# Block-sparse attention in the last batch of an attention-then-gMLP kernel, with key blocks and value rows gathered by register addresses

## The chip, the cores and the metric

The kernel runs on one core of one Trainium2 chip. The metric is device time in microseconds (us) of one execution, as the median of the runs shown. "Span" is the time from the first to the last instruction in one profiled execution. The engines go by the profile's names: PE (TensorE; PEld are its weight loads), DVE (VectorE), ACT (ScalarE), POOL (GpSimd), SP (SyncE, which here only issues DMAs).

## What is computed

Attention of 4 batches with 8 heads each (768 positions, 64 values a head) under a mask made of blocks of 32 positions, and behind it a gMLP block whose spatial product mixes all 768 positions of a batch. There are 24 query blocks and 24 key blocks:

```python
B, H, S, D = q.shape                       # 4, 8, 768, 64
mask = np.abs(blk_i - blk_j) <= 1
mask = mask | (blk_i == 0) | (blk_j == 0) | (blk_i == n_blocks - 1) | (blk_j == n_blocks - 1)
for qb in range(n_blocks):
    for kb in sampled_blocks[qb]:          # 3 drawn block numbers for each query block
        mask[qb * block:(qb + 1) * block, kb * block:(kb + 1) * block] = True
scores = np.where(mask, scale * np.matmul(q, k.transpose(0, 1, 3, 2)), -1e9)
attn = softmax(scores)                     # exp, divided by its sum
x = np.matmul(attn, v)                     # heads side by side: 4 x 768 x 512
h = np.maximum(x @ w_in, 0.0)              # d_ff = 1024
u, v = h[..., :512], h[..., 512:]
v_n = (v - mean(v)) / np.sqrt(var(v) + 1e-06)
v_s = np.einsum('ts,bsd->btd', w_spatial, v_n) + b_spatial[None, :, None]
out = (u * v_s) @ w_out
```

An inner query block may look at its own block and its two neighbours, at the first and the last key block, and at three drawn blocks: 8 of the 24, fewer where some coincide. The first and the last query block look at all 24. The drawn numbers are an input, so they are known only on the chip.

## The kernel before

**Staging.** Heads are worked in pairs: pair p is batch p // 4, heads 2(p % 4) and the next, so batch b has pairs 4b to 4b + 3. `load` (line 106) brings k, q and v of a pair from memory on SP's queue as [128, 2, 384] fp32; `cast` (118) turns them to bf16 on POOL, v into `vv`; `tr_dma` (372) transposes the pair's k and q with one DMA transpose on SP; `split` (376) copies one head from there into `kq[head]` on DVE. `kq` (line 83) holds 8 heads of keys and queries, 64 rows of values and under them rows that carry the mask: a product of keys and queries adds the penalty of a forbidden block by itself, so all 24 key blocks are computed for each query block.

**Slots.** An order written out by hand runs over slots s (loop at line 846). Batch 0 takes slots 0 to 35 in another form. From slot 36 (`S0`) on, each slot does one `qk_full` (422): for one head and one chunk of 128 keys, two products into PSUM (512 and 256 queries, line 428) and one exp on ACT over 128 x 768 (431) into the tile `a_all`. Seven slots later (`LAG`) `av_full` (471) multiplies: six products of 65 columns (values and a column of ones) for one chunk of 128 queries (line 476). A pair takes 12 slots, `slot_of(p) = 36 + 12 (p - 4)`; so the last batch, pairs 12 to 15, has slots 132 to 179. After six chunks `normalize` (438) divides on DVE; `xtr_dma` (507) transposes the pair's result by DMA on SP, after which the gMLP can read it.

**gMLP.** The gMLP of batch b (class `Moe`, 571) is a list of 108 steps, each one product of 512 columns or two of 256: 48 for `in_steps`, 36 for the spatial product, 24 for the last one. `deal` and `run_queue` spread it over 48 slots. Batch 2's list starts at slot 144, inside the last batch's attention; batch 3's runs alone at the end (line 867). In `v_product` DVE computes mean and variance, POOL the reciprocal root (`std`, `rstd`, lines 598 and 600), and DVE scales `vn` with it; the spatial product reads `vn`. `o_product` (669) issues the output DMA on SP (682).

**Order.** `when(slot, ...)` puts work into a slot (lines 808 to 837). Each engine's queue is in program order; a wait holds all that stands behind it on that engine. SP carries all loads, DMA transposes and outputs. A DMA waits until the one eight places before it, which uses the same semaphore, has landed.

Of the kernel before, what the change touches and what calls it, by code (L numbers as in the profile page):

```python
# [26 lines left out]
def kernel(  # L27
# [16 lines left out]
    nc = tc.nc  # L44
# [27 lines left out]
    psum = ctx.enter_context(tc.tile_pool(name="psum", bufs=1, space=bass.MemoryType.PSUM))  # L72
    ctx.enter_context(tc.manual_schedule())
# [8 lines left out]

    kq = const.tile([128, H, 2 * S], BF16, name="kq")
    NVV = 6
    vv = [const.tile([128, 2, NCH, VA], BF16, name=f"vv{s}") for s in range(NVV)]
# [20 lines left out]
    def load(p, nm, hs=BOTH, cs=ALLC, eng=nc.sync):  # L106
        if (nm, p) not in st:
            st[nm, p] = work.tile([128, 2, S // 2], FP32, tag="st_" + nm, bufs=4 if nm == "q" else 3, name="st_" + nm)
        eng.dma_start(out=st[nm, p][:, hs, cs.start * D:cs.stop * D],
                      in_=dram(SRC[nm], p, hs, cs))  # L110
# [7 lines left out]
    def cast(p, nm, eng, hs=BOTH, cs=ALLC):  # L118
        if nm == "v":
            dst = vv[p % NVV][:, hs, cs, 0:D]  # L120
        else:
            if p not in nat:
                nat[p] = work.tile([128, 2 * NCH, 2, D], BF16, tag="nat", bufs=4, name="nat")
            c0 = 0 if nm == "k" else NCH
            dst = nat[p][:, c0 + cs.start:c0 + cs.stop].rearrange("p c h d -> p h c d")[:, hs]
        src = st[nm, p].rearrange("p h (c d) -> p h c d", d=D)[:, hs, cs]
        if p == 0 and nm != "v":
            dst = nat0_view()[:, hs, (c0 + cs.start) * D:(c0 + cs.stop) * D]
            if cs is not C45:
                dst = dst[:, 0].rearrange("p (i t d) -> p t i d", t=2, d=D)  # L130
                src = src[:, 0].rearrange("p (t i) d -> p t i d", t=2)
            else:
                dst = dst.rearrange("p h (c d) -> p h c d", d=D)
        if eng is nc.scalar:
            nc.scalar.activation(out=dst, in_=src, func=AF.Copy)
        else:
            eng.tensor_copy(out=dst, in_=src)  # L137
# [13 lines left out]
    hot = const.tile([128, NCH, 128], BF16)  # L151
    lim = const.tile([128, NCH, 128], BF16)
# [65 lines left out]

    def w_load(key, src):
        wst[key] = work.tile([128, DM], FP32, tag="osb", bufs=6, name="w_f")  # L220
        nc.sync.dma_start(out=wst[key], in_=src)
# [160 lines left out]


# [3 lines left out]
    def qk_unit(u, e):  # L387
        if e == 0:
            a_ref[u] = work.tile([128, NCH * S], BF16, tag="a_all", bufs=3,
                                 name="a_all")[:, 0:2 * NCH * TW]  # L390
# [31 lines left out]
    def qk_full(j, ci):  # L422
        if ci == 0:
            a_ref["h", j] = work.tile([128, NCH * S], BF16, tag="a_all", bufs=3,
                                      name="a_all").rearrange("p (c n) -> p c n", c=NCH)
        ps = psum.tile([128, 1024], FP32, tag="sc", bufs=2)
        for n0, n1 in ((0, 512), (512, S)):
            nc.tensor.matmul(out=ps[:, n0:n1],  # L428
                             lhsT=kq[:, j % H, ci * 128:(ci + 1) * 128],
                             rhs=kq[:, j % H, S + n0:S + n1], start=True, stop=True)  # L430
        nc.scalar.activation(out=a_ref["h", j][:, ci, :], in_=ps[:, 0:S], func=AF.Exp, scale=0.125)  # L431
# [80 lines left out]

    ws = {}

    def ws_load(i):
        ws["f", i] = work.tile([128, S], FP32, tag="ws_f", bufs=6, name="ws_f")
        nc.sync.dma_start(out=ws["f", i],
                          in_=moe_w_spatial.rearrange("(p c) s -> c p s", c=NCH)[i])

    def b_load():  # L520
        ws["b_nat"] = work.tile([128, S], FP32, tag="ws_f", bufs=6, name="b_nat")
        nc.sync.dma_start(out=ws["b_nat"], in_=moe_b_spatial.partition_broadcast(128))
# [5 lines left out]
    def ws_cast(i):  # L528
        if i % 2 == 0:
            ws["b", i // 2] = work.tile([128, 2, NCH, 128], BF16, tag="ws_b", bufs=2, name="ws_b")  # L530
# [40 lines left out]
    class Moe:  # L571
# [97 lines left out]
        def o_product(self, tcc, n):  # L669
# [4 lines left out]
            for i in range(parts):  # L674
                cs = slice(i * w, (i + 1) * w)

                def done(ps, i=i, cs=cs):
                    if i == 0:
                        osb["t"] = work.tile([128, DM], FP32, tag="osb", bufs=6, name="osb")
# [105 lines left out]
    def last_x():  # L785
# [13 lines left out]
        xt = xt_tile(NP - 1)  # L799
        for cs in (slice(0, TW), slice(TW, S)):  # L800
            dve_copy(xt[:, cs], ps[:, cs])
# [9 lines left out]
    for p in range(NG, NP):  # L811
        g = slot_of(p)
        when({4: 14, 5: 20, 6: 28, 11: g - 29, 15: g - 29}.get(p, g - 36), c(load, p, "k"), c(load, p, "q"), c(load, p, "v"))
        when({4: 17, 5: 23, 6: 37, 11: g - 22, 15: g - 22}.get(p, g - 24),
             *[c(cast, p, nm, PL, cs=cs) for nm in "kqv" for cs in (((C01, C23, C45) if p > 5 else (ALLC,)))])
        when({4: 21, 5: 27, 11: g - 18, 15: g - 18, 10: g - 17, 14: g - 17}.get(p, g - 19), c(tr_dma, p))
# [5 lines left out]
        if p == NP - 1:  # L822
            when(g + 20, last_x)
        elif p % NG == NG - 1:
# [13 lines left out]

    LAG = 7
    av_at = {}  # L840
# [5 lines left out]
    for s in range(NS + LAG + 2):  # L846
        if s < S0:
            qk_unit(*divmod(s, 3))
        elif s < NS:
# [7 lines left out]
        if 0 <= s - LAG - S0 and s - LAG < NS:  # L857
# [40 lines left out]
```

## Time and profile before

| what | value |
|---|---|
| runs (us) | 210.04, 210.03, 210.24; median 210.04 |
| span of the profiled execution | 208.3 us, granted clock 1.000 |
| the execution's own time | not on the page; 210.04 - 208.3 = 1.7 us is taken as what lies around the span |
| busy share of the span | PE 97%, PEld 66%, DVE 70%, ACT 81%, POOL 43% |
| DMA | 53053 packets, 39.48 MB, mean 190 GB/s |

A busy PE means that some matmul is under way; matmuls are pipelined, so the time that one costs is read from start to start. In a group's row "busy" is the union of its instructions, "mean ns" the length of one. Rows with "SPq" are instructions of SP's own sequencer: their length is the time for which the queue is held. A row of one line's instructions gives min/median/max in ns and the first and last start in us.

### The profile page before, as it was taken

The numbers are of one execution on the slowest core, as the hardware profiler recorded it, in microseconds if no ns is written. First come the engines' busy times: TensorE is split into PE (matmuls) and PEld (weight loads), VectorE is DVE, ScalarE is ACT, GpSimd is POOL, SyncE is SP. The second block draws the span as 40 slices with busy tenths as digits, with TensorE's granted clock in tenths as the row PEclk, the third lists the DMA queues.
The fourth block names the chain that finished last, engine by engine and source line by source line (L and its number), as shares of the span: only waits on it lengthen the run. The fifth ranks groups of instructions, "written<-read, shape, count | busy, mean of one in ns | idle before, by whom it ended". The sixth has DMA issues, their size and how long they took to land.

```text
span 208.3 us, 5489 instructions
## 1 busy us (share of the span) xinstructions
PE 201.0 (97%) x2203; PEld 138.0 (66%) x2225; DVE 146.8 (70%) x315; ACT 168.4 (81%) x222; POOL 89.4 (43%) x186
## 2 busy tenths in 40 slices
PE   6899999999999999999999999999999999999993
PEld 6599888777766776667556676667665567445551
DVE  6888776989876766575975585456875666576871
ACT  6899999999999999989899878889899884266021
POOL 6888989767927964006757600006210000013000
PEclk9999999999999999999999999999999999999999
DMA  5999899999999999499987920499402010610016
GB/s 143 338 362 357 275 383 270 206 247 389 253 253 308 259 300 208 139 199 386 292 176 206 139 41 0 164 189 335 75 0 41 0 37 4 250 57 0 0 70 232
DMA packets 53053, 39.48 MB, mean 190 GB/s; under 512 B 33956, under 2 KB 47652, under 8 KB 53028
## 3 DMA queue, kind: packets, MB, share of 16 engines
q1 hardware_dynamic: 52596, 38.74, 70.0%
q10 hardware_dynamic: 432, 0.39, 0.6%
q8 instruction: 17, 0.28, 0.5%
q14 instruction: 8, 0.07, 0.1%
HBM read 24.77 MB, written 6.29 MB: 149 GB/s over the span
## 4 chain that ended last, share of the span: by engine, by line
PE 87%; DVE 4%; ACT 4%; DMA 2%; issue 1%; POOL 0%; ACTq 0%
PE ps L428 21%; PE ps_moe L630 17%; PE ps_moe L561 13%; PE ps_av L476 12%; PE ps L415 7%; PE ps_av L458 4%; PE ps_t L561 4%; PE ps_t L630 4%; PE ps_sc L630 2%; ACT a_all L420 2%; DVE stats L594 2%; DVE vn L185 2%; DMA st_q<-in_q_dram 2%; PE ps_sc L561 1%; PE ps L263 1%
## 5 line engine op out<-in xcount | busy, mean ns | idle before, releaser
L431 ACT ACTIVATE a_all<-ps 128x768 bf16<-128x768 f32 x144 | 113.4, 812 | 13.8 <-PE ps L428 6.2
L428 PE MATMUL ps<-kq 128*128 128x512 bf16 (+1 forms) x288 | 70.3, 326 | 0.3
L476 PEld LDWEIGHTS <-a_all 128*128 128x128 bf16 x864 | 46.6, 98 | 19.0
L476 PE MATMUL ps_av<-vv,a_all 128*128 128x65 bf16 x864 | 51.1, 194 | 0.1
L428 PEld LDWEIGHTS <-kq 128*128 128x128 bf16 x288 | 27.9, 97 | 23.6
L137 POOL CAST nat<-st_k 128x256 bf16<-128x256 f32 (+3 forms) x37 | 17.7, 509 | 38.7 <-DMA st_k<-in_k_dram 38.7
L420 ACT ACTIVATE a_all<-ps 128x1024 bf16<-128x1024 f32 x35 | 33.5, 1027 | 0.3
L630 PE MATMUL ps_moe<-w_spt,vn 128*128 128x512 bf16 (+1 forms) x144 | 33.1, 325 | 0.0
L598 POOL TENSOR_SCALAR std<-mv 128x3 f32<-128x3 f32 (+1 forms) x9 | 3.4, 376 | 48.7 <-DVE mv L595 48.5
L661 DVE TENSOR_TENSOR sb<-ps_moe,b_row 128x512 f32<-128x512 f32 x18 | 12.4, 690 | 14.5 <-PE ps_moe L630 14.2
L630 PE MATMUL ps_moe<-xt,w_in_t 128*128 128x256 bf16 (+1 forms) x108 | 21.7, 299 | 0.2
L415 PE MATMUL ps<-kq 128*128 128x256 bf16 x135 | 20.8, 275 | 0.8 <-DVE kq L211 0.6
L561 PE MATMUL ps_moe<-w_in_t,xt 128*128 128x512 bf16 x65 | 20.2, 378 | 0.2
L137 POOL CAST vv<-st_v 128x256 bf16<-128x256 f32 (+2 forms) x37 | 18.5, 533 | 3.9 <-DMA st_v<-in_v_dram 3.8
L137 POOL CAST nat<-st_q 128x256 bf16<-128x256 f32 (+2 forms) x41 | 19.2, 496 | 1.6 <-DMA st_q<-in_q_dram 1.5
L561 PE MATMUL ps_moe<-w_out_t,un 128*128 128x512 bf16 x64 | 19.4, 378 | 0.2
L441 DVE TENSOR_TENSOR xn<-ps_av,rc 128x384 bf16<-128x384 f32 (+1 forms) x36 | 18.5, 513 | 1.4 <-DVE rc L440 0.2
L664 DVE TENSOR_TENSOR un<-sb,un 128x512 bf16<-128x512 f32 x24 | 17.4, 727 | 1.5
L630 PEld LDWEIGHTS <-vn 128*128 128x128 bf16 x192 | 15.5, 97 | 4.4
L594 DVE BATCH_NORM_STATS2 stats<-vn 128x6 f32<-128x512 bf16 x24 | 16.5, 688 | 1.5 <-ACT vn L589 0.9
L211 DVE COPY osb<-ps_moe 128x512 f32<-128x512 f32 x12 | 8.3, 689 | 11.2 <-PE ps_moe L561 9.3
L211 DVE COPY kq<-tt 64x1536 bf16<-64x1536 bf16 x24 | 15.4, 641 | 0.6 <-DMA tt<-nat 0.2
(94 smaller groups left out, 241.6 us busy)
## 6 DMA issues: line engine op xcount, KB each, us to landing
out_dram<-osb SPq DMA_DIRECT2D x23, 256.0 KB, 2.1
st_k<-in_k_dram SPq DMA_DIRECT2D x15, 384.0 KB, 4.6
st_v<-in_v_dram SPq DMA_DIRECT2D x15, 384.0 KB, 6.2
st_q<-in_q_dram SPq DMA_DIRECT2D x12, 384.0 KB, 4.9
ws_f<-in_moe_w_spatial_dram SPq DMA_DIRECT2D x6, 384.0 KB, 5.5
w_f<-in_moe_w_in_dram SPq DMA_DIRECT2D x8, 256.0 KB, 6.3
w_f<-in_moe_w_out_dram SPq DMA_DIRECT2D x4, 256.0 KB, 5.4
st_q<-in_q_dram SPq DMA_DIRECT2D x3, 256.0 KB, 6.9
```

Of the source, the lines that this page charges most:

```text
L137: eng.tensor_copy(out=dst, in_=src)
L211: nc.vector.tensor_copy(out=o, in_=i)
L415: nc.tensor.matmul(out=ps[:, at:at + n * TW], lhsT=kq[:, h, ci * 128:(ci + 1) * 128], rhs=kq[:, h, qcols(t0, n)], start=True, stop=True)
L420: nc.scalar.activation(out=out, in_=ps, func=AF.Exp, scale=0.125)
L428: nc.tensor.matmul(out=ps[:, n0:n1], lhsT=kq[:, j % H, ci * 128:(ci + 1) * 128], rhs=kq[:, j % H, S + n0:S + n1], start=True, stop=True)
L431: nc.scalar.activation(out=a_ref["h", j][:, ci, :], in_=ps[:, 0:S], func=AF.Exp, scale=0.125)
L441: nc.vector.tensor_tensor(out=out, in0=ps[:, :, 0:D], in1=rc[:, 0:n].to_broadcast([128, n, D]), op=ALU.mult)
L476: nc.tensor.matmul(out=av_ref[j][:, qc, :], lhsT=a_ref["h", j][:, ci, qc * 128:(qc + 1) * 128], rhs=vv[p % NVV][:, h, ci, :], start=(ci == ...
L561: nc.tensor.matmul(out=ref["ps"][:, 0:w], lhsT=lhs(i), rhs=rhs(i), start=(i == 0), stop=(i == n - 1))
L594: nc.vector.bn_stats(out=stats, in_=self.vn[:, tcc, :])
L630: nc.tensor.matmul(out=o.rearrange("p (c t) -> p c t", c=n), lhsT=lhs(i)[:, (d0 + x) * 128:(d0 + x + 1) * 128], rhs=rhs(i), start=(i == 0) ...
L664: nc.vector.tensor_tensor(out=self.in_place(*area), in0=sb, in1=self.in_place(*area), op=ALU.mult)
```

## The change

Pairs 12 to 15 leave the dense path; batches 0 to 2 keep it.

- **Keys.** k and q are cast for two pairs at a time and transposed with four DMA transposes (`tr_dma2`). `k_natural` brings the keys of a pair (both heads on 128 rows) into natural order (`kt`); `k_pairs` and `k_edges` copy the neighbours and the first and last blocks to their places, on DVE for pairs 12 and 13 and on ACT for 14 and 15. `k_sampled` loads block numbers into POOL registers and copies 32 columns for each of 22 inner query blocks x 3 draws, once for pairs 12 and 13 and once for 14 and 15: 132 register loads and 132 copies of 128 x 2 x 32.
- **Queries.** `q_split` builds `q2`, in which each head's queries stand beside zeros for the other head, so that one product over 128 rows gives both heads.
- **Values.** v of the four pairs is cast into `vnat` and written to a scratch in device memory (`v_rows_out`: rows of 8 heads x 65, 1040 bytes). From there `v_window` and `v_edges` read the fixed rows with 4 + 1 and 2 + 3 + 2 DMAs, and `v_sampled` reads the drawn ones: 22 x 3 DMAs on SP of 32 rows each (33 KB), each with its address from a register of SP. They land in the old bytes of `kq`, `st_v` and `st_k`.
- **Products.** For each pair `sp_qk` issues 11 products of 128 columns (kind "f": two neighbouring query blocks), 22 of 64 (kind "x": the sampled blocks) and 6 of 128 (kind "d": first and last query block), with 9 exps of together 3584 columns; `sp_av` issues 78 products of 65 columns, 4 slots later (`SLAG`). `a_zero` clears what no exp writes.
- **After.** `x_order` puts the result back into the order of the other batches, on ACT, for the last pair half on DVE. `osb` has 4 buffers, not 6; staging tiles become parts of tiles that are used again.

```diff
+    def sample_index(raw, r, d, e, n):
...
+        ts(sidx["k"].rearrange("o (n r) -> o n r", n=NX), r, 1.0, ALU.mult)
...
+        tt_op(sidx["v"].rearrange("o (n r) -> o n r", n=NX), r, e, ALU.add)
+    def values(nm, i0, n, eng, top):
+        return nc.values_load_multi_w_load_instructions(
+            sidx[nm][0:1, i0:i0 + n], engines=[eng], min_val=0, max_val=top,
+            skip_runtime_bounds_check_because="block numbers")[1]
+    def v_rows_out():
+        nc.sync.dma_start(out=scr[0:S].rearrange("(p c) w -> p c w", c=NCH),
+                          in_=vnat.rearrange("p c h d -> p c (h d)"))
+    def v_window(part):
+        s = nc.sync.dma_start
+        n = NF - 1
+        if part == 0:
+            s(out=vf[0:2 * BLK, 0:n], in_=by_blocks(3 * BLK, n))
+            s(out=vf[0:2 * BLK, n], in_=scr[BLK:3 * BLK])
+            for p0, row in ((2 * BLK, 0), (3 * BLK, S - BLK)):
+                s(out=vf[p0:p0 + BLK],
+                  in_=scr[row:row + BLK, None, :].to_broadcast([BLK, NF, VW]))
+        elif part == 1:
+            s(out=vd, in_=scr[0:S].rearrange("(c p) w -> p c w", c=NCH))
+    def v_sampled(x0, n):
+        vals = values("v", x0 * NR, n * NR, mybir.EngineType.SP, S)
+        for i, val in enumerate(vals):
+            x, r = x0 + i // NR, i % NR
+            nc.sync.dma_start(out=vx(x)[(r + 1) * BLK:(r + 2) * BLK],
+                              in_=scr[bass.ds(val, BLK)])
+    def k_natural(i, copy):
+        src = tt["k", i // 2][:, i % 2 * NCH:(i % 2 + 1) * NCH]
+        copy(kt(i).rearrange("x (p c) -> x c p", c=NCH), src)
+    def k_sampled(g, x0, n):
+        vals = values("k", x0 * NR, n * NR, mybir.EngineType.Pool, S - BLK)
+        src = kt_cols[:, 2 * g * S:2 * (g + 1) * S].rearrange("x (i t) -> x i t", i=2)
+        for j, val in enumerate(vals):
+            x, r = x0 + j // NR, j % NR
+            nc.gpsimd.tensor_copy(out=xk[:, 2 * g:2 * g + 2, x, (r + 1) * BLK:(r + 2) * BLK],
+                                  in_=src[:, :, bass.ds(val, BLK)])
+    def q_split(i, h, copy):
+        rs = slice(h * D, (h + 1) * D)
+        src = tt["q", i // 2][rs, i % 2 * NCH:(i % 2 + 1) * NCH]
+        dst = q2[i % 2][rs, h]
+        n = (128 - P0) * NCH
+        copy(dst[:, 0:n].rearrange("x (p c) -> x c p", c=NCH), src[:, :, P0:128])
+        copy(dst[:, n:S].rearrange("x (p c) -> x c p", c=NCH), src[:, :, 0:P0])
+    def tr_dma2(nm, g):
+        tt[nm, g] = work.tile([128, 2 * NCH, 128], BF16, tag="tt", bufs=2, name="tt")
+        nc.sync.dma_start_transpose(out=tt[nm, g],
+                                    in_=nat.pop((nm, g)).rearrange("p c h d -> p (c h d)"))
+    T = slot_of(PS)
...
+    for nm, p, ld, ca in (("v", 12, 84, 92), ("v", 13, 86, 93), ("k", 12, 88, 96), ("k", 13, 90, 98),
+                          ("v", 14, 93, 100), ("v", 15, 96, 103), ("q", 12, 99, 107), ("q", 13, 102, 109),
+                          ("k", 14, 112, 118), ("k", 15, 115, 122), ("q", 14, 124, 131), ("q", 15, 127, 134)):
+        when(ld, c(load, p, nm))
+        when(ca, c(cast, p, nm, PL))
+    when(105, v_rows_out, c(tr_dma2, "k", 0))
+    when(T - 23, c(v_window, 0))
...
+    for j in range(6):
+        n = 4 if j < 5 else 2
+        when(115 + 3 * j, c(k_sampled, 0, 4 * j, n))
+    when(118, c(tr_dma2, "q", 0))
+    for i in range(2):
+        for h in range(2):
+            when(122 + 4 * i + 2 * h, c(q_split, i, h, dve_copy))
+    when(114, c(v_sampled, 12, 4))
+    when(116, c(v_sampled, 16, 4), c(v_edges, 1))
+    when(T - 11, c(v_sampled, 0, 3))
+    when(T - 8, c(v_sampled, 3, 2), c(tr_dma2, "k", 1))
+    when(T, c(v_edges, 0), c(v_sampled, 5, 4))
+    when(T + 2, c(v_sampled, 9, 3))
+    when(T + 4, c(v_edges, 2), c(v_window, 1), c(v_sampled, 20, 2))
...
+    for j in range(6):
+        n = 4 if j < 5 else 2
+        when(T + 5 + 3 * j, c(k_sampled, 1, 4 * j, n))
+    when(T + 6, c(tr_dma2, "q", 1))
...
-    for s in range(NS + LAG + 2):
-        if s < S0:
+    for s in range(NS + LAG):
+        if s >= T:
+            if s < NS:
+                sp_qk(*divmod(s - T, 12))
+        elif s < S0:
...
+        if 0 <= s - SLAG - T < NS - T:
+            sp_av(*divmod(s - SLAG - T, 12))
```

`T` is 132. `sp_av` of a pair takes six query chunks in turn: the first five need four of the sampled blocks each (x0 to x3, x4 to x7, and so on to x19), the sixth needs x20, x21 and `vd`.

More of the change, by code (lines that the diff above doesn't have):

```diff
@@ new lines, in x_order, with xtr_sp @@
+    def x_order(p, src, lo, hi, copy):
+        dst = xt_tile(p).rearrange("x (c p) -> x c p", c=NCH)
+        cut = 128 - P0
+        for a, b in ((lo, min(hi, cut)), (max(lo, cut), hi)):
+            if a < b:
+                d0 = (a + P0) % 128
+                copy(dst[:, :, d0:d0 + b - a],
+                     src[:, a * NCH:b * NCH].rearrange("x (p c) -> x c p", c=NCH))
+    def xtr_sp(p):
+        nc.sync.dma_start_transpose(
+            out=xtn.rearrange("p (c n) -> p c n", c=NCH),
+            in_=xn_ref.pop(("p", p)).rearrange("p c h d -> p (c h d)"))
@@ L798, in last_x @@
             tr(ps, cc, pair_of(xn, cc))
-        xt = xt_tile(NP - 1)
-        for cs in (slice(0, TW), slice(TW, S)):
-            dve_copy(xt[:, cs], ps[:, cs])
+        x_order(NP - 1, ps, 0, 64, dve_copy)
+        x_order(NP - 1, ps, 64, 128, act_copy)
         for f in seq[2 * NG:2 * NG + n]:
```

311 lines of the change are left out of this document (288 added, 23 removed).

## The prediction

> **What bounds the kernel now.** I read the three 48-slot stretches from slot 36 on first (engine columns: busy us and count), then the shares of the chain of waits.
>
> ```profile
> core 0: us, PE busy (x) PEld busy (x) DVE busy (x) ACT busy (x) POOL busy (x), PEclk, DMA share, GB/s
> 45.20:93.00 47.80, 47.59 (x557) 32.29 (x562) 34.89 (x64) 44.37 (x59) 26.07 (x53) 1.00 1.04 250
> 93.00:141.00 48.00, 47.63 (x506) 30.93 (x511) 31.59 (x64) 41.98 (x57) 16.93 (x40) 1.00 0.73 182
> 141.00:189.00 48.00, 47.73 (x471) 30.22 (x473) 32.55 (x70) 35.18 (x50) 6.94 (x15) 1.00 0.29 83
> ...
> PE 87%; DVE 4%; ACT 4%; DMA 2%; issue 1%; POOL 0%; ACTq 0%
> ```
>
> PE is busy all the time in each stretch and carries 87% of the chain; the others have room. So a product taken from PE is worth its start-to-start time, as long as nothing makes PE wait. The timeline of PE in the last batch gives those prices (start, length):
>
> ```profile
> 158.44 0.49 PE L428 MATMUL ps<-kq 128*128 128x512 bf16 x2
> 158.77 0.36 PE L476 MATMUL ps_av<-vv,a_all 128*128 128x65 bf16 x6
> 158.96 0.38 PE L630 MATMUL ps_moe<-xt,w_in_t 128*128 128x512 bf16 x1
> 159.18 0.59 PE L630 MATMUL ps_moe<-w_spt,vn 128*128 128x512 bf16 x2
> 159.61 0.49 PE L428 MATMUL ps<-kq 128*128 128x512 bf16 x2
> ```
>
> The two score products (768 columns) hold PE for 158.77 - 158.44 = 0.33 us, six value products for 0.19 (0.032 each), a gMLP step for (159.61 - 159.18) / 2 = 0.215. A slot of the last batch is 0.33 + 0.19 + 108 / 48 x 0.215 = 1.00 us: the step list of 48 slots fits the 48 us of the stretch. PE has no gap to give.
>
> **What the products save.** Between 65 columns at 32 ns and 512 at 215, 128 columns cost 57 ns; 64 cost 32. A pair needs 17 x 0.057 + 22 x 0.032 + 78 x 0.032 = 4.2 us instead of 12 x 0.52 = 6.2: 2.0 saved, 8.0 for four pairs, and a slot of the last batch becomes 0.835 us. The 32 ns include 864 hidden weight loads, so I count the new loads at nothing; uncovered, at the 98 ns of the next rows, the 39 score products would cost 3.8 us a pair in place of 1.7, and the saving would be gone.
>
> ```profile
> L476 PEld LDWEIGHTS <-a_all 128*128 128x128 bf16 x864 | 46.6, 98 | 19.0
> L431 ACT ACTIVATE a_all<-ps 128x768 bf16<-128x768 f32 x144 | 113.4, 812 | 13.8 <-PE ps L428 6.2
> L420 ACT ACTIVATE a_all<-ps 128x1024 bf16<-128x1024 f32 x35 | 33.5, 1027 | 0.3
> L648 ACT ACTIVATE un<-ps_moe 128x512 bf16<-128x512 f32 x12 | 7.1, 592 | 0.0
> L211 DVE COPY kq<-tt 64x1536 bf16<-64x1536 bf16 x24 | 15.4, 641 | 0.6 <-DMA tt<-nat 0.2
> ```
>
> **ACT and DVE.** 812 and 1027 ns give 0.84 ns a column and 0.17 fixed. Nine exps with 3584 columns cost 4.5 us a pair against 9.7. The copies that ACT takes on (keys and queries of pairs 14 and 15, `x_order`) are at the same rate about 15 us, and batch 2's relu and output copies 5.4 (nine of some 0.6): 18 + 15 + 5.4 = 38.6 us in a stretch of 40.1. That hides, barely; I take 0, bounds 0 and +2. DVE loses eight `split` copies (5.1 us) and gains copies and clears of about the same sum; with 31.6 busy of 48 that is hidden too, as are the index arithmetic and the casts on POOL.
>
> **SP's queue.** The gathers add 66 DMAs to one queue. Each holds SP until its issue is done:
>
> ```profile
> L682 SPq DMA_DIRECT2D out_dram<-osb x24: 332/333/439, 79.6 to 204.9; - x24
> DMA to landing us min/median/max: 2.0/2.1/5.5
> ...
> L109 SPq DMA_DIRECT2D st_q<-in_q_dram x20: 368/468/914, 2.1 to 137.7; - x20
> ...
> L142 SPq DMA_DIRECT2D samp<-in_sampled_blocks_dram x1: 445/445/445, 0.7 to 0.7; - x1
> ...
> L508 SPq DMA_TRANSPOSE xt<-xn x11: 1209/1233/2024, 63.4 to 169.6; - x11
> ...
> L374 SPq EVENT_SEMAPHORE  x12: 17/22/28, 26.6 to 140.6; - x12
> L374 SPq DMA_TRANSPOSE tt<-nat x12: 1423/2166/5675, 28.4 to 143.3; - x12
> ...
> DMA to landing us min/median/max: 4.0/5.2/9.3
> ...
> L440 DVE RECIPROCAL rc<-ps_av x36: 150/184/198, 12.2 to 178.1; 128x6 f32<-128x6 f32 x24, 128x4 f32<-128x4 f32 x12
> ```
>
> The cheapest issue is 0.33 us with 128 rows, and 0.45 with 24 rows of 24 bytes (L142): fewer rows did not make it shorter. The next rows show 0.04 us between two issues (46.42 + 0.47 to 46.93). A static gather would cost 0.37. The register load and the address arithmetic are not in the trace. Below, they are two sequencer instructions like the semaphore's, 2 x (0.017 + 0.04) = 0.11; above, a load as slow as a small POOL operation (0.37, in the last rows below) and more arithmetic, 0.5. I take 0.19, the length of the reciprocal, the nearest row of something that fetches a few elements from SBUF. So c = 0.56 us a gather. If the issue did scale with rows, a quarter of 0.33 and 0.11 would give c = 0.23; the upper end is 0.9.
>
> When the queue reaches the gathers, and when they are needed, comes from the transposes of finished pairs, which leave as soon as slot 102 (pair 8), 114, 126 (pair 10) and 138 are done:
>
> ```profile
> 46.42 0.47 SPq L109 DMA_DIRECT2D st_q<-in_q_dram  x1
> 46.93 0.47 SPq L109 DMA_DIRECT2D st_v<-in_v_dram  x1
> ...
> 98.54 1.71 SPq L508 DMA_TRANSPOSE xt<-xn  x1
> ...
> 109.02 1.21 SPq L508 DMA_TRANSPOSE xt<-xn  x1
> ...
> 121.49 1.21 SPq L508 DMA_TRANSPOSE xt<-xn  x1
> ```
>
> Slot 126 begins near 120 and slot 132 near 126 us. SP is past pair 8's transpose at 100.3; `v_rows_out`, the first `tr_dma2`, the landing of the rows and the four of `v_window` bring it to 104.3. From there it isn't held by slots, only by what it waits for, and the targets are free early. Up to the last gather it issues four loads (2.0), seven of `v_edges` and one of `v_window` (3.0), two transposes at 2.2 and two at 1.27, one output (0.4), together 12.3, and 66 x 0.56 = 37.0. The end is 104.3 + 12.3 + 37.0 = 153.6, landed at 155.7. Value products for the last query chunk of pair 12 stand at slot 145, without a wait at 126 + 13 x 0.835 = 136.9. They come 18.8 us late, and PE takes its queue in order, so everything behind them does: the rest of batch 2's gMLP, pairs 13 to 15 and the tail.
>
> The same queue hurts once before: the queries' transpose stands behind 24 gathers. It is issued at 104.3 + 24 x 0.56 + 4 = 122 and lands at 129, while `q_split` stands in DVE's order at slot 122 (116 us). Behind it wait `normalize` and the gMLP's evictions, so PE runs out of PSUM at about 121. This only moves slot 132 to near 135; SP, which itself comes to `v_edges(0)` at about 135, still sets the end, so nothing is added.
>
> **Two rules.** The Trainium skill's page "DMA: Bandwidth & Descriptors" (section "Issuing engines are not separate DMA queues") says that the sequencer's time to start a DMA is usually small relative to the DMA. By that rule there would be no late gather and the time would be 202 us; here 0.33 stands against 2.1, and 66 of them are 22 us. Its page "Runtime: NRT & Kernel Launch" (section "Instruction fetch mechanics") prices a register load at about 200 ns, in bulk too; no run here shows one. By that, and one address instruction, c would be 0.63 and the time 225.
>
> **POOL.** 132 gathers of 64 elements, with no row for either part:
>
> ```profile
> 141.16 1.09 POOL L137 CAST nat<-st_k 128x256 bf16<-128x256 f32 x3 [21.77 <-DMA st_k<-in_k_dram]
> 2.75 0.42 POOL L171 MEMSET vv<- 128x12 bf16 x6
> L598 POOL TENSOR_SCALAR std<-mv 128x3 f32<-128x3 f32 (+1 forms) x9 | 3.4, 376 | 48.7 <-DVE mv L595 48.5
> ```
>
> A cast of 256 elements takes 0.36 in a row of three, a memset of 12 0.07. I put a gather at g = 0.35 (0.18 copy, 0.17 register), bounds 0.18 and 0.7. The second 66 start when q of pair 15 is cast, near 139, and end at 162. Behind them in POOL's order stands `std` of batch 2, needed by DVE at about slot 157, on my timeline 155.7 + 12 x 0.835 = 165.7. Hidden by SP's lateness, up to g = 0.40.
>
> **Sum.** 208.3 - 8.0 + 18.8 = 219.1 us of span, with 1.7 around it 221.
>
> **Rivals.**
> 1. *Cheap gathers.* Below c = 0.40 SP's lateness no longer eats the 8.0 (26.2 us of room over 66). For it: short rows, and no load or address is shown. Against: 0.37 is already there without them. At c = 0.23, and with POOL under 0.28, nothing is late: 208.3 - 8.0 + 1.7 = 202. The Trainium skill's page "DMA: Bandwidth & Descriptors" (same section) would put it here. Chance 0.20, spread from 202 to 209.6.
> 2. *POOL is the bound.* From g = 0.40 the reciprocal roots of batch 2 come after DVE asks for them; at g = 0.7 the second 66 end at 185, 19.5 late on top of the forecast: 240. For it: one engine does load, arithmetic and copy in one order. Against: small POOL operations overlap (six memsets in 0.42). Chance 0.15, from 224 to 243.
> 3. *The change doesn't lighten PE*, since short products show their weight loads: 8 us more, 229. Against: 864 loads under 65 columns are hidden. Chance 0.03.
> 4. *Gain and lateness cancel*, c = 0.40: 210. Chance 0.03.
>
> The forecast, SP's queue sets the end, has 0.59, from 211 (c = 0.42) to 235 (c = 0.77). A measurement of this kernel tells 0.2% (0.4 us) from no change. Faster 0.20; within 0.2% 0.03; slower 0.77. The likeliest case's own range is 212 to 233; the range that also takes in most of the others is 203 to 240.
>
> **What would show it.** SP's rows of the new gather line: 66 issues, and a period of about 0.56 us while it isn't waiting; a period under 0.40 proves me wrong. PE in the stretch from 121 to 157 should show gaps that end on DMAs into the value rows, DVE one that ends on the queries' transpose; PE and ACT should be near their full loads again afterwards, with 0.835 us a slot. POOL's copies should be 0.35 apart, and `rstd` should not end a wait of DVE. If PE stays at 9 tenths throughout and the span is near 200, SP's queue was never the point; if the gap sits at `vn`, it was POOL.

## The result and the profile after

| | before | changed |
|---|---|---|
| median, us (lowest to highest of 4 runs) | 210.03 (209.74 to 210.24) | 272.25 (270.71 to 272.84) |
| span of the profiled execution, us | 208.3 | 271.1 |
| PE busy, us | 201.0 | 214.3 |
| PE idle between its first and its last product, us (span - 4.6 - busy) | 2.7 | 52.2 |

The ratio is 1.295 (95%: 1.291 to 1.299). The forecast was 221, range 203 to 240: the direction is right, and the time lies far outside the range. The 4.6 us are what lies before PE's first product (1.0) and behind its last (3.6). The 62.8 us of span are 49.5 of PE standing still and 13.3 of PE being busy longer, although by the prediction's prices it has 8 us less to do.

The page of the changed kernel: span, busy times, PE's busy tenths and its granted clock in 40 slices of 6.8 us, then the chain of waits.

```profile
span 271.1 us, 6355 instructions
...
PE 214.3 (79%) x2309; PEld 144.1 (53%) x2309; DVE 162.6 (60%) x352; ACT 173.3 (64%) x242; POOL 113.7 (42%) x302
...
PE   8899999999299988979602974582939479999994
...
PEclk9999999999959999999955795978689959999999
...
PE 50%; SPq 13%; DMA 11%; DVE 11%; ACT 7%; issue 5%; POOL 1%; ACTq 0%; DVEq 0%; POOLq 0%
```

The three stretches that were read of before, and the one that follows them (the same columns):

```profile
45.20:93.00 47.80, 41.91 (x460) 28.04 (x459) 33.30 (x72) 36.48 (x49) 29.05 (x66) 0.93 0.94 247
93.00:141.00 48.00, 36.46 (x383) 22.45 (x380) 26.74 (x60) 32.55 (x44) 29.50 (x88) 0.95 0.92 217
141.00:189.00 48.00, 26.02 (x264) 16.46 (x264) 22.74 (x36) 18.57 (x28) 14.09 (x68) 0.75 0.60 133
189.00:237.00 48.00, 36.78 (x439) 24.79 (x438) 22.16 (x46) 32.30 (x53) 2.23 (x4) 0.84 0.13 25
```

No engine is full in any of them; the work waits in turns. PE was 87% of the chain and is now 50%. The stops begin in slice 11 (from 68 us), and behind nearly every stop the clock digit falls to 5 to 8. PE's groups with the idle time ahead of them say who ended the stops:

```profile
line engine op names shapes xcount | busy us, mean ns | idle before us <-releasers
L971 PE MATMUL ps_moe<-w_spt,vn 128*128 128x512 bf16 (+1 forms) x144 | 37.1, 351 | 21.0 <-DVE sb L1002 20.7 <-DVE vn L211 0.2
...
L902 PE MATMUL ps_moe<-w_in_t,xt 128*128 128x512 bf16 x72 | 24.7, 409 | 7.0 <-DMA xt<-xn 7.0
...
L827 PE MATMUL ps_av<-kq,a_all 128*128 128x65 bf16 x184 | 15.4, 212 | 4.0 <-DMA kq<-v_rows 4.0
...
L755 PE MATMUL ps<-oh,ws 128*128 128x64 bf16 x44 | 3.0, 204 | 5.1 <-DMA kq<-v_rows 4.8
...
L755 PE MATMUL ps<-oh,kt 128*128 128x128 bf16 x12 | 1.8, 277 | 5.6 <-ACT a_all L762 5.6
L755 PE MATMUL ps<-st_q,kt 128*128 128x128 bf16 x12 | 1.7, 261 | 5.1 <-ACT a_all L762 5.1
```

Two rows name the gathered rows. The 4.0 are value products, which read them. The 4.8 are score products, which don't: that product began at 166.53, just as an exponential of ACT (165.91, 0.57 long) ended, which stood behind a copy of keys. Of DVE's 20.7, two stops are 20.0 (5.81 us at 69 and 14.17 at 133), and DVE itself was waiting in both (its timeline, idle time and releaser in brackets):

```profile
68.85 0.27 DVE L211 TENSOR_SCALAR ws<-ws 1x66 f32<-1x66 int32 x1 [5.38 <-DMA ws<-in_sampled_blocks_dram]
...
74.10 0.31 DVE L214 TENSOR_TENSOR vi<-ws 1x66 int32<-1x66 f32 x1
...
145.44 1.44 DVE L237 COPY oh<-tt 64x672 bf16<-64x672 bf16 x2 [15.42 <-DMA tt<-nat]
```

At 69 us it waited for the 66 block numbers and then spent 5.6 us on them; at 130 us it waited for the queries' transpose. SP's timeline shows why that came late:

```profile
95.96 1.35 SPq L542 DMA_TRANSPOSE xt<-xn  x1
...
109.06 1.34 SPq L542 DMA_TRANSPOSE xt<-xn  x1
110.50 0.52 SPq L623 DMA_DIRECT2D v_rows<-ws  x1
...
116.55 0.75 SPq L633 DMA_DIRECT2D kq<-v_rows  x1
...
120.87 9.76 SPq L660 DMA_DIRECT2D st_v<-v_rows  x12
...
141.68 1.48 SPq L718 DMA_TRANSPOSE tt<-nat  x1
145.28 1.92 SPq L660 DMA_DIRECT2D kq<-v_rows  x4
...
151.80 2.88 SPq L660 DMA_DIRECT2D kq<-v_rows  x6
...
178.11 4.19 SPq L660 DMA_DIRECT2D st_k<-v_rows  x6
...
185.93 1.26 SPq L542 DMA_TRANSPOSE xt<-xn  x1
```

Between 120.9 and 182.3 us the queue holds the 66 gathers, and all else on SP stands between or behind them: the queries' transpose at 141.68, pair 11's at 185.93 (before: 133.87), for which PE stops 4.93 us. What a gather costs SP:

```profile
L660 SPq FUSED_REGOPS  x66: 37/37/51, 120.7 to 181.9; - x66
L660 SPq MOVE kq<-v_rows x36: 29/29/34, 145.2 to 174.8; - x36
L660 SPq DMA_DIRECT2D kq<-v_rows x36: 315/316/348, 145.3 to 174.9; - x36
```

```profile
L610 SPq TENSOR_LOAD <-vi x7: 753/1277/2487, 119.7 to 177.2; - x7
```

(Minimum, median, maximum in ns.) Six gathers in a row take 2.88 us, so the period is (2.88 - 0.32) / 5 = 0.51; seven register loads with a median of 1.28 add 7 x 1.28 / 66 = 0.14: c = 0.65 us. Where a gather must wait for an earlier one to land, it is longer: the first 12 took 9.76.

Last, ACT in the first of two like stops (195.9 to 200.8, and again 213.1 to 218.7 us):

```profile
192.10 2.76 ACT L240 ACTIVATE oh<-tt 64x672 bf16<-64x672 bf16 x2
194.48 0.80 ACT L789 ACTIVATE a_all<-ps 128x512 bf16<-128x512 f32 x1
195.18 1.63 ACT L240 ACTIVATE a_all<-kt 128x640 bf16<-128x640 bf16 x4
196.83 2.74 ACT L240 ACTIVATE oh<-tt 64x672 bf16<-64x672 bf16 x2
...
200.09 0.65 ACT L762 ACTIVATE a_all<-ps 128x256 bf16<-128x256 f32 x2
```

The exponential PE waits for stands behind 4.4 us of copies in ACT's order.

### The profile page after: what moved, and what is told of

Its sections match the earlier page's. It is cut to its first block, busy times and chain, and to the rows that moved or that the text cites. A ratio compares the mean times of both kernels' runs of the same rounds, so it can differ in the third digit from the quotient of the medians.

```text
span 271.1 us, 6355 instructions
## 1 busy us (share of the span) xinstructions
PE 214.3 (79%) x2309; PEld 144.1 (53%) x2309; DVE 162.6 (60%) x352; ACT 173.3 (64%) x242; POOL 113.7 (42%) x302
## 4 chain that ended last, share of the span: by engine, by line
PE 50%; SPq 13%; DMA 11%; DVE 11%; ACT 7%; issue 5%; POOL 1%; ACTq 0%; DVEq 0%; POOLq 0%
PE ps_moe L902 9%; PE ps_moe L971 7%; PE ps L462 6%; SPq L660 6%; PE ps L450 5%; DMA xt<-xn 4%; DMA st_k<-in_k_dram 3%; PE ps_av L510 3%; PE ps_av L492 3%; PE ps_t L902 3%; PE ps_t L971 3%; DMA st_k<-v_rows 2%; PE ps_av L827 2%; PE ps L755 2%; SPq L610 2%
## 5 line engine op out<-in xcount | busy, mean ns | idle before, releaser
L465 ACT ACTIVATE a_all<-ps 128x768 bf16<-128x768 f32 x96 | 75.1, 812 | 38.9 <-PE ps L462 34.1
L971 PE MATMUL ps_moe<-w_spt,vn 128*128 128x512 bf16 (+1 forms) x144 | 37.1, 351 | 21.0 <-DVE sb L1002 20.7
L462 PE MATMUL ps<-kq 128*128 128x512 bf16 x192 | 49.3, 340 | 0.1
L510 PEld LDWEIGHTS <-a_all 128*128 128x128 bf16 x576 | 32.4, 102 | 13.2 <-issue 1.9
L510 PE MATMUL ps_av<-vv,a_all 128*128 128x65 bf16 x576 | 35.6, 199 | 0.0
L902 PE MATMUL ps_moe<-w_in_t,xt 128*128 128x512 bf16 x72 | 24.7, 409 | 7.0 <-DMA xt<-xn 7.0
L699 POOL COPY ws<-kt 128x64 bf16 x132 | 26.2, 253 | 5.1 <-ACT kt L240 3.7
L462 PEld LDWEIGHTS <-kq 128*128 128x128 bf16 x192 | 19.1, 101 | 17.3 <-issue 3.4
L211 DVE TENSOR_SCALAR vn<-ps_moe 128x512 bf16<-128x512 f32 x18 | 12.3, 686 | 18.6 <-PE ps_moe L902 18.6
L450 PE MATMUL ps<-kq 128*128 128x256 bf16 (+1 forms) x136 | 21.0, 276 | 1.0 <-DVE kq L237 0.8
L163 POOL CAST nat<-st_k 128x256 bf16<-128x256 f32 (+3 forms) x29 | 14.9, 542 | 13.3 <-DMA st_k<-in_k_dram 11.6
L827 PE MATMUL ps_av<-kq,a_all 128*128 128x65 bf16 x184 | 15.4, 212 | 4.0 <-DMA kq<-v_rows 4.0
```

The lines of the kernel that those rows point to most:

```text
L450: nc.tensor.matmul(out=ps[:, at:at + n * TW], lhsT=kq[:, h, ci * 128:(ci + 1) * 128], rhs=kq[:, h, qcols(t0, n)], start=True, stop=True)
L462: nc.tensor.matmul(out=ps[:, n0:n1], lhsT=kq[:, j % H, ci * 128:(ci + 1) * 128], rhs=kq[:, j % H, S + n0:S + n1], start=True, stop=True)
L510: nc.tensor.matmul(out=av_ref[j][:, qc, :], lhsT=a_ref["h", j][:, ci, qc * 128:(qc + 1) * 128], rhs=vv[p % NVV][:, h, ci, :], start=(ci == ...
L699: nc.gpsimd.tensor_copy(out=xk[:, 2 * g:2 * g + 2, x, (r + 1) * BLK:(r + 2) * BLK], in_=src[:, :, bass.ds(val, BLK)])
L827: nc.tensor.matmul(out=av_ref["s"][:, 2 * c + h, :], lhsT=a_cols[:, at - off:at - off + 128], rhs=heads(rows_v, 2 * i + h), start=start, s ...
L902: nc.tensor.matmul(out=ref["ps"][:, 0:w], lhsT=lhs(i), rhs=rhs(i), start=(i == 0), stop=(i == n - 1))
```

## The experiments

Each kernel is the changed kernel with one or more edits, run once beside a run of the kernel before (209.9 to 210.7 us). The changed kernel's four runs lie within 2.1 us, so smaller differences say nothing. x2, x3, x7, x10 and x12 leave work out or read other blocks, so their results are not the reference's.

| run | what | us | difference | PE idle / busy |
|---|---|---|---|---|
| x1_index | index arithmetic spread over slots | 270.66 | -1.6 | 54.1 / 210.2 |
| x2_few | no value gathers | 252.68 | -19.6 | 39.0 / 207.0 |
| x3_static | no register addresses | 264.94 | -7.3 | 49.1 / 209.6 |
| x4_copies_dve | copies on DVE | 257.58 | -14.7 | 45.5 / 205.8 |
| x5_q_first | queries' transpose first | 271.87 | -0.4 | 58.1 / 207.6 |
| x6_three | x1 + x4 + x5 | 256.40 | -15.9 | 45.5 / 204.7 |
| x7_three_few | x6 + x2 | 230.56 | -41.7 | 23.0 / 201.0 |
| x8_warm | idle products ahead of two stops | 264.66 | -7.6 | 43.8 / 214.6 |
| x9_two_queues | x6, gathers on SP and ACT | 242.14 | -14.3 to x6 | 31.8 / 204.0 |
| x10_few_k | x7, no key gathers on POOL | 234.02 | +3.5 to x7 | 25.7 / 201.7 |
| x12_no_zero | x7, no clears | 231.30 | +0.7 to x7 | 23.0 / 201.6 |
| x13_late_loads | x9, later loads | 245.48 | +3.3 to x9 | 32.8 / 206.3 |

**x1_index: is the stop at 69 us a loss of its own?**

```diff
     def sample_index(raw, r, d, e, n):
+        steps = []
+
+        def ts(*x):
+            steps.append(lambda: ts_now(*x))
...
+        for k_, f in enumerate(steps):
+            when(68 + k_, f)
```

> The arithmetic on the sampled block numbers is the same, but DVE does its 25 operations one per slot from slot 68 on, instead of all in slot 62. Theory A (this is a stop of its own): PE's gap of 5.81 us at 69.3 us goes, because DVE no longer waits 5.38 us for the load of the numbers in front of the gMLP's evictions; the time falls by about 5.8 us, from 272.3 to about 266.5. Rival (SP's queue alone sets the end, and an earlier DVE only waits longer for it): the gap at 69 goes, those from 133 us on grow by as much, and the time stays within 1.5 us of 272.

`sample_index` still stands in slot 62, but there it only puts its operations into later slots (19 of them in the trace; the expectation counts 25). The stop at 69 went, and a new one of the same size came 25 us later (PE's timeline):

```profile
100.46 1.04 PE L914 MATMUL ps_moe<-w_in_t,xt 128*128 128x512 bf16 x2 [6.00 <-DMA xt<-xn]
```

The rival holds in the time, though not in the place it named: the next late item was pair 7's transpose, which SP issued at 91.4 behind seven loads and four outputs (before: 86.2).

**x2_few: what do the value gathers cost?**

```diff
 def v_sampled(x0, n):
+        for a, m, t in vx_parts:
+            lo, hi = max(a, x0), min(a + m, x0 + n)
+            if lo < hi:
+                nc.sync.dma_start(out=t[BLK:(NR + 1) * BLK, lo - a:hi - a],
+                                  in_=scr[0:NR * BLK, None, :].to_broadcast([NR * BLK, hi - lo, VW]))
+        return
```

> Leaves out the 66 value gathers from SP's queue: three to eight larger transfers from fixed rows fill the same places, so the value rows are other rows than the reference's; no register loads on SP. Theory A (SP's queue is the largest part): the gaps of PE that end on SP's transfers go, 14.2 us at 133, 4.5 us between 172 and 183, 4.9 us at 184, and some of the half-speed clock behind them: 272 falls to 240 to 249. Rival (ACT's strided copies and the stop at slot 62 are the larger part, and the queue is hidden behind them): the gaps at 69, 162, 196 and 213 stay and others grow, and the time stays above 258.

252.7, between the two expectations: the same bytes in seven transfers instead of 66 are worth 19.6 us. The stops on gathered rows are gone, that on pair 11's transpose fell to 0.70 us, and the 14.17 at 133 became 6.04 and 3.09. Those on ACT stay (5.85 and 5.60 us), and that at 69 too. PE's idle time fell by 13.2 us and its busy time by 7.3.

**x3_static: the register part of it.**

```diff
 def values(nm, i0, n, eng, top):
+        return [BLK * ((7 * (i0 + i)) % NB) for i in range(n)]
```

> Rows and columns of the gathers (on SP and on POOL) are taken from fixed addresses instead of registers, the same number and the same size of transfers and copies; the blocks gathered are other blocks than the reference's. Theory A (the register loads and the address arithmetic are a third of SP's 0.60 us a gather, and SP's queue sets the end up to 182 us): the period of the gathers falls to about 0.4 us, 66 of them take 13 us less, and the time falls by 8 to 13 us, to 259 to 264. Rival (the queue is late by what it waits for and by the transposes and loads in it, not by its period): at most 4 us, 268 to 272.

-7.3 us, just short of theory A's 8 to 13, and about a third of what leaving out the gathers brings. But its period of 0.4 us did not come. On SP (one line's row, then the timeline):

```profile
L661 SPq DMA_DIRECT2D kq<-v_rows x36: 314/419/820, 141.7 to 167.3; - x36
...
146.77 2.73 SPq L661 DMA_DIRECT2D kq<-v_rows  x6
```

An issue with a fixed address holds SP for 0.42 us, one with a register for 0.316, and the two address instructions ahead of it (37 and 29 ns) make up for most of that: six take 2.73 us in place of 2.88. What went from SP is the register loads, about 9 us at 1.28 each. (POOL's went with them.)

**x4_copies_dve: ACT's strided copies.**

```diff
-        when(T + 2 * i - 4, c(k_natural, i, act_copy))
+        when(T + 2 * i - 4, c(k_natural, i, dve_copy))
...
-            when(T + 12 * (i - 1) + 3 + 2 * h, c(q_split, i, h, act_copy))
+            when(T + 12 * (i - 1) + 3 + 2 * h, c(q_split, i, h, dve_copy))
```

> The copies of the keys and the queries of pairs 14 and 15 (four rows of about 2.75 us on ACT) are given to DVE; nothing else changes. Theory A (ACT's strided copies hold the exponentials): the gaps of 4.81 us at 162, 4.87 at 196 and 5.60 at 213 shrink to below 1 us each, and the time falls by 10 to 15 us to 257 to 262. Rival (SP's queue sets the end): the two gaps at 196 and 213 lie after the last gather and may go, but the one at 162 turns into a wait for the gathers; at most 10 us, and if DVE, which then holds the evictions, takes ACT's place, nothing: 262 to 272.

-14.7: theory A in the time. The stops at 196 and 213 went; that at 162 only shrank to 3.23. PE's idle time fell by 6.7 us and its busy time by 8.5. DVE does the same two copies of a head in 1.45 us where ACT took 2.76:

```profile
190.26 1.45 DVE L237 COPY oh<-tt 64x672 bf16<-64x672 bf16 x2
```

**x5_q_first: does the late transpose of the queries count?**

```diff
-    when(118, c(tr_dma2, "q", 0))
+    when(111, c(tr_dma2, "q", 0))
```

> The first transpose of the queries is put at slot 111 instead of 118, so that it stands ahead of the first 24 gathers in SP's queue instead of behind them. Theory A (that transpose being late stops DVE, DVE stops PE, PE stops SP, which gives the 14.2 us gap at 133 us): the gap goes and is not made up later, since SP too goes on sooner; 272 falls to 256 to 260. The prediction's own reading (the late transpose only moves slot 132 and the queue sets the end in any case): the gap at 133 goes and the waits on gathers between 172 and 184 grow by about as much; 268 to 272.

The prediction's own reading held in the time, though not in the place: the waits on gathers did not grow. The gap at 133 went, and a larger one (21.11 us at 147) came, because the next item in the same queue was late, the keys' second transpose (ACT's timeline):

```profile
143.26 0.60 ACT L783 ACTIVATE a_all<-ps 128x512 bf16<-128x512 f32 x1
160.72 2.75 ACT L240 ACTIVATE kt<-tt 128x768 bf16<-128x768 bf16 x1 [16.86 <-DMA tt<-nat]
```

**x6_three and x7_three_few: do the parts add up?**

> The three single changes together: the index arithmetic dealt over slots, the copies of pairs 14 and 15 on DVE, the queries' first transpose ahead of the gathers. Theory A (SP's queue still sets the end at the first value products, the copies on ACT cost about 15 us behind it, and the other two only move waits): the sum of the three measured alone, -1.6 -14.7 -0.4 us, so about 255. Rival (each of the stops hid the next one, and with two of them gone the third counts too): 240 to 250.

> As the three together, and with the 66 value gathers left out for a few large transfers from fixed rows (the value rows are other rows than the reference's). Theory A (queue, index load, late transpose and ACT's copies are all that is lost): the sum of the four alone, 272.3 - 36.3 = 236, or less where they covered each other, down to 215, and PE's gaps sum up to less than 15 us. Rival (another cause that none of the four touches, such as transfers that share the 16 DMA engines, or POOL's copies of keys): above 236, with gaps of PE behind POOL or behind transposes that were issued in time and landed late.

x6: the sum of its parts (-16.7 expected, -15.9 measured). x7: -41.7, five more than the four alone (-36.3), so they covered each other a little. Its 230.6 meets theory A's sum, but not its limit on the gaps: 23.0 us of PE idle are left, where 15 was the bound. Most of it is 7.0 us at 90 to 99 (osb's output, then pair 7's transpose; osb has 4 buffers here where it had 6, and no run gave them back), 7.5 at 136 to 149 (three stops of 2.56, 1.71 and 3.23, ended by DVE, DVE and ACT) and 2.4 behind `vn`.

**x8_warm: the clock.**

```diff
 def sp_av(i, e):
...
+                spare["t"] = ps
...
+            if i in (1, 2) and (qd, h, stop) == (1, 0, True):
+                for _ in range(80):
+                    nc.tensor.matmul(out=spare["t"][:, 400:512], lhsT=ident, rhs=ident[:, 0:112],
+                                     start=True, stop=True)
```

> The changed kernel with 160 idle matmuls more: 80 of 112 columns (about 4 us together) after the third group of value products of pair 13 and of pair 14, that is just ahead of PE's gaps of 4.87 us at 195.9 and 5.60 us at 213.1; they write columns that nobody reads. Theory A (the granted clock falls to a half for some 3 to 5 us because PE stood still before): PE no longer stands still there, the granted clock between 201 and 206 us (0.68) and between 219 and 224 us (0.50) stays at 1.0, and the time falls by 3 to 4 us, 272.3 to about 269, although PE has more to do. Rival (the clock falls for another reason): the clock in these stretches stays low, and the time stays or grows by up to 8 us.

With 160 more products the kernel is 7.6 us faster, where theory A expected 3 to 4. The stretches of the changed kernel (columns as above); the last is the 5 us behind the second of the two stops:

```profile
201.00:206.00 5.00, 5.00 (x52) 3.18 (x51) 2.06 (x5) 2.48 (x5) 0.35 (x2) 0.68 0.01 2
...
218.74:223.74 5.00, 5.00 (x38) 3.06 (x38) 1.07 (x3) 2.55 (x6) 0.00 (x0) 0.50 0.00 0
```

and the same with the idle products:

```profile
201.00:206.00 5.00, 4.59 (x73) 3.05 (x73) 4.74 (x12) 3.56 (x5) 0.59 (x1) 1.00 0.01 2
...
213.35:218.35 5.00, 4.81 (x65) 3.10 (x65) 1.96 (x5) 4.07 (x8) 0.00 (x0) 1.00 0.01 3
```

Without them PE is busy all of these 5 us and gets 38 products done at half the clock; with them it is 65 from the same point of the program on. From the end of the stop at 184 to the end of the program it is 82.2 us without and 77.2 with them, so 5.0 of the 7.6 lie in the part that was edited; the other 2.6 are little more than the scatter. The Trainium skill's page "TensorE: Matmul & The Clock Gate" (Part 1) states that after an idle window of about 3.4 us the clock is halved until PE was busy for one such window; these rows agree: behind stops of 4.87 and 5.60 us the clock is 0.68 and 0.50, and with PE kept busy it is 1.00.

**x9_two_queues: is it the number of issues on one engine?**

```diff
 def v_sampled(x0, n):
...
+        for eng, dma, a, b in ((mybir.EngineType.SP, nc.sync, 0, m),
+                               (mybir.EngineType.Activation, nc.scalar, m, n * NR)):
+            for i, val in enumerate(values("v", x0 * NR + a, b - a, eng, S), a):
...
```

> The three changes together (256.4 us), and of each call's gathers the second half is started by ACT instead of SP, with its own register loads; same number, same bytes. Theory A (what makes the gathers late is the time that one engine needs to start 66 of them): SP's stretches of gathers halve, the waits on value rows between 169 and 175 us and a part of the gap of 16 us at 142 go, and the time falls by 10 to 16 us, to 240 to 246. Rival (ACT's issues and register loads stand in front of the exponentials, 33 times 0.5 us): the gaps end on ACT's results instead, and the time is 252 us or more.

-14.3 with the same transfers and bytes: theory A, and more than half of what leaving them out brought (25.8). The rival's price shows too, in ACT's timeline:

```profile
119.11 0.81 ACT L465 ACTIVATE a_all<-ps 128x768 bf16<-128x768 f32 x1 [0.73 <-PE ps L462]
121.03 3.39 ACTq L674 DMA_DIRECT2D st_v<-v_rows  x6
124.53 0.81 ACT L465 ACTIVATE a_all<-ps 128x768 bf16<-128x768 f32 x1 [4.61 <-POOL ws L713]
```

Six issues and their register load hold the next exponential 4.61 us back. The releaser named there, POOL, was inferred; the row between the two exponentials is what filled the time. PE's idle time ended by these exponentials is 7.2 us in all. 242.14 is the fastest kernel of this study that leaves no work out, and far from 210: no version run beats the kernel before.

**x10_few_k and x12_no_zero: POOL and DVE in what is left.**

```diff
 def k_sampled(g, x0, n):            # x10
+        for i in (2 * g, 2 * g + 1):
+            nc.gpsimd.memset(xk[:, i, x0:x0 + n, BLK:(NR + 1) * BLK], 0.0)
+        return
 def a_zero(n, lo, hi, eng):         # x12
-        eng.memset(a_cols[:, n * AW + lo:n * AW + hi].bitcast(FP32), 0.0)
+        pass
```

> As the three together with the value gathers left out (230.6 us), and with POOL's 132 copies of sampled key columns left out for 24 larger clears (the sampled keys are zeros) and without POOL's register loads. Theory A (POOL is off the path, as the prediction had it with g below 0.40): within 1.5 us of 230.6. Rival (POOL's copies hold the score products, or hold up DVE): PE's gaps between 136 and 149 us (7.5 us in all) shrink, 223 to 227.

> As the three together with the value gathers left out (230.6 us), and without the three clears of the probability buffers on DVE (1.98, 1.98 and about 0.4 us; the buffers keep old probabilities, so the sums are others than the reference's). Theory A (between 136 and 149 us DVE has more to do than the slots give it: four copies of the queries, two of the keys, the clears and the gMLP's evictions, and PE's gaps of 2.56 and 1.71 us there are DVE's): the gaps shrink and the time falls by 3 to 5 us, to 226 to 228. Rival (DVE waits there for transposes, not for itself): at most 1 us.

Neither made it faster, and neither is a clean answer. x10 was 3.5 us slower, outside both expectations. The 24 clears that it puts in place of POOL's copies are work of their own: while 12 of them run (139.57 to 143.62), DVE's two copies of a head take 4.73 us instead of 1.46, and the stop of 3.73 at 142 ends on DVE right behind them. So x10 doesn't show that POOL's copies cost nothing; it shows that these stops are there without them. In x12 two of the three stops went, since both were waits for a clear, one through DVE's order and one through ACT. The second in x7 (ACT's timeline), where the clear ran from 146.13 to 148.11:

```profile
148.21 0.60 ACT L801 ACTIVATE a_all<-ps 128x512 bf16<-128x512 f32 x1 [2.19 <-DVE a_all L758]
```

The one at 143 grew to 3.20, because DVE's copy of the keys now waits for their transpose (DVE's timeline in x12):

```profile
144.24 1.46 DVE L237 COPY kt<-tt 128x768 bf16<-128x768 bf16 x1 [1.43 <-DMA tt<-nat]
```

PE's idle time in all stayed 23.0 us: the stop at 94 grew to 6.12 as well, and others came.

**x13_late_loads: are the loads brought forward the cause of the stops at 90 to 99?**

```diff
-    for nm, p, ld, ca in (("v", 12, 84, 92), ("v", 13, 86, 93), ("k", 12, 88, 96), ("k", 13, 90, 98),
-                          ("v", 14, 93, 100), ("v", 15, 96, 103), ("q", 12, 99, 107), ("q", 13, 102, 109),
+    for nm, p, ld, ca in (("v", 12, 92, 99), ("v", 13, 93, 100), ("k", 12, 95, 102), ("k", 13, 96, 103),
+                          ("v", 14, 94, 101), ("v", 15, 100, 106), ("q", 12, 99, 107), ("q", 13, 102, 109),
...
-    when(105, v_rows_out, c(tr_dma2, "k", 0))
+    when(107, v_rows_out, c(tr_dma2, "k", 0))
```

> The kernel with the gathers on two queues (242.1 us), with the loads of values and keys of pairs 12 and 13 put 6 to 8 slots later, value rows of pair 15 four slots later, and the output of the value rows at slot 107 instead of 105. Theory A (the loads that the change brings forward stand ahead of the transpose of pair 7 and share its DMA engines, and that gives PE's gaps of 1.93 us at 90 and 5.30 us at 94): these two gaps go, and the time falls by 4 to 7 us, to 235 to 238. Rival (the later loads make the value rows and with them the gathers later by as much): the gap at 94 goes, those at 122 to 152 grow, and the time stays above 240.

The rival in the time, though not by its path: the stop at 94 fell from 5.30 to 1.67 us, so the loads do make that transpose late, but a new one of 4.24 appeared at 112, where DVE waits for the keys' first transpose, and the time is 3.3 us longer. The gaps from 122 to 152 hardly grew. DVE's timeline:

```profile
113.97 1.45 DVE L237 COPY kt<-tt 128x768 bf16<-128x768 bf16 x1 [3.54 <-DMA tt<-nat]
```

## Why the prediction failed

**PE's products: right.** In x7, at full clock, the four 128-column products and six value products take (start, length)

```profile
182.80 0.39 PE L773 MATMUL ps<-st_q,vv 128*128 128x128 bf16 x4
183.02 0.22 PE L845 MATMUL ps_av<-st_v,a_all 128*128 128x65 bf16 x2
...
183.20 0.60 PE L989 MATMUL ps_moe<-w_spt,vn 128*128 128x512 bf16 x2
```

(183.02 - 182.80) / 4 = 0.055 and (183.20 - 183.02) / 6 = 0.030 us, against 0.057 and 0.032. The weight loads stay hidden, and rival 3 falls. By these prices the 8.0 us are there; they are buried.

**SP's queue: right in size, in part by luck.** c is 0.65 instead of 0.56. The 0.19 for load and address came out, as 0.14 and 0.05 (0.51 - 0.46); what was too low is the issue with a fixed address, taken at 0.37 and in x3 (2.73 - 0.42) / 5 = 0.46 from start to start. The chain began at 119.7 (the first register load), not 104.3, because SP was past pair 8's transpose only at 110.4 instead of 100.3 and then waited for the rows to land; it lasted 62.6 us, not 49.3. The term of the sum was 18.8, and removing the gathers gave 19.6. But the 18.8 were to be PE's wait at the gathered rows, and these waits are under 5 us in all. The rest came through transposes that stand among and behind the gathers, and 7.3 us of what x2 gains is PE's busy time, a term that the sum doesn't have. That the queries' transpose adds nothing by itself was right too (x5: -0.4), though its stop was 14 us, where slot 132 was to move by 9 (126 to 135). Rivals 1 and 4 needed c at 0.40 or less. By the Trainium skill's rule that starting a DMA takes little ("DMA: Bandwidth & Descriptors", section "Issuing engines are not separate DMA queues") the forecast would have been 202, and the rows speak against it. By the Trainium skill's 200 ns for a register load ("Runtime: NRT & Kernel Launch", section "Instruction fetch mechanics") c was 0.63, near the 0.65 measured, though not by that share: the load is 0.14 a gather here.

**POOL: right.** 132 copies took 26.2 us, 0.20 each where 0.35 was taken with the register loads, and DVE's waits for `rstd` are 3.5 us in all, the longest 1.3: rival 2 falls.

**ACT: the step that failed.** "That hides, barely; I take 0, bounds 0 and +2" cost 14.7 us. Two errors are in it. The copies were priced at the exponentials' 0.84 ns a column, "about 15 us"; they took 26: two of 2.76 for the keys, four of 2.75 for the queries, 4.3 for `x_order` and 5.2 for the pairs and edges. 672 columns in 2.44 us are 3.6 ns a column. And the room was read as a share of 40 us, where the copies of a pair stand in a bunch ahead of the exponentials PE needs next: 4.4 us there are a stop, whatever the share. In x4, 6.7 us of the gain are PE's idle time and 8.5 its busy time.

**DVE and SP's other customers: the same error in small.** "Hidden ... as are the index arithmetic" left out where DVE would wait for its input: a stop of 5.81 us. Moving it alone gained nothing that can be told, as the late transposes behind the loads took its place (x1).

**The clock: missing from the sum.** PE was busy 214.3 us where 201.0 - 8.0 = 193.0 were due. In x7, with 23 us of stops in place of 52, it is 201.0. The clock explains most of the surplus. The seven stretches of the changed kernel in which the granted clock was one half, added up (length, then busy us of each engine):

```profile
sum 51.20, PE 33.00 PEld 20.43 DVE 21.09 ACT 17.31 POOL 12.52; mean PE 4.71 PEld 2.92 DVE 3.01 ACT 2.47 POOL 1.79
```

33.0 us of PE's busy time lie in them, and in x7 10.8 in two such stretches. By an estimate that takes half of these as lost, that is 16.5 of the 21.3 us and 5.4 of the 8.0; for the rest no run gives a cause. A long stop is paid for again behind it, and a sum that turns waits into microseconds one for one is too low.

So of the 70.8 us between the span of 271.1 and the 200.3 that would be the saving alone, the gathers, ACT's copies, the index and the queries' transpose explain 42.3 together (x7's span is 228.8). Of the 28.5 left, 20.3 are stops beyond the 2.7 of before and 8.0 PE's longer busy time. Between 136 and 149 us two stops are waits for the clears and one stands behind a copy of keys on DVE (x12); but no run turned them into time, so what these 28.5 us are worth one by one stays open.

## What to carry to other kernels

Where an in-order engine is given new work, count it in the slots just ahead of what the busiest engine waits for, not as a share of a long stretch, and price a copy by a row with the same access pattern. A queue of many small transfers is paid in issue time on its engine, and everything behind it, transposes above all, comes late by that much. Add the clock to every stop of some 5 us: by the estimate above, stops cost a quarter to a third of their length again (5.4 us on 20.3 in x7, 16.5 on 49.5 in the changed kernel). Removing one stop can leave the time as it is, since the next late item takes its place (x1, x5, x12).

## What the hardware showed

- Strided bf16 copies are slow on ACT: 2.76 us for the two of a head (64 partitions, 672 and 96 columns) against 1.45 on DVE.
- Register loads are a cost per load more than per register. SP's seven, of 6, 9 or 12 values, took 0.75 to 2.49 us. On POOL ten loads of 12 values and two of 6 differ little (ns):

```profile
L610 POOLq TENSOR_LOAD <-ki x12: 800/810/1033, 123.0 to 176.5; - x12
```

- In the changed kernel the granted clock is 0.50 in seven stretches, together 51 us; six of them are 3.4 or 6.8 us long, one 17.1. A stop of 3.20 us was enough in x12 (clock 0.50 from 146.1 to 152.9), one of 3.23 at 184 in x4 was not.
- POOL's gathers in x7 (ns: minimum, median, maximum):

```profile
L717 POOL COPY ws<-kt x132: 228/233/3761, 122.0 to 165.0; 128x64 bf16 x132
```

The longest of them started at 145.7 us, when DVE cleared 128x2304 (146.13 to 148.11) and copied keys (148.03 to 149.42). Without the clears (x12) the longest is 1.53 us, and 30 copies take 8.60 us instead of 12.57. The page "SBUF — State Buffer" of the Trainium skill (section "SBUF: two separate sides") says that DVE, for some of its instructions, and GpSimd take one shared port pair exclusively, each for a whole instruction. That fits, and so does x10's DVE copy beside POOL's clears; which of DVE's instructions here are of that kind, no trace shows.
